# A chunked state-space scan and two feed-forward layers on one core: scores of three tiles from rounded terms, and two edits at the start

## The chip, the cores and the metric

The kernel runs on one NeuronCore of a Trainium2 chip. The metric is the device time of one execution in microseconds (us); lower is better. TensorE (PE) multiplies matrices into PSUM, VectorE (DVE) and ScalarE (ACT) work elementwise, GpSimd (POOL) does a little, SyncE (SP) only issues transfers; ScalarE has a transfer queue of its own.

## The reference

Three stages, each feeding the next, all in float32 from outside:

```python
# 1. chunked scan, per sequence b (4) and head h (8); S=768, D=32, N=16
L = exp(cum_i - cum_j) * causal          # cum: cumulated log a
M = (C_i . B_j) * L                      # the "scores" C_i . B_j, contraction of 16
y = M @ x + (C @ state) * exp(cum)
state = decay * state + sum_j B_j x_j * decay_from_j
# 2. x = y of all heads (3072 x 256)
xn = x / sqrt(mean(x*x) + 1e-6) * rms_g
x2 = (silu(xn @ w_gate) * (xn @ w_val)) @ w_out          # 256 -> 1536 -> 256
# 3. mixes x2 with the row before it
k = relu(xk @ w_k);  v = (k*k) @ w_v;  out = sigmoid(xr @ w_r) * v
```

## The kernel before

The 768 positions are cut into six tiles of 128 (tile c = 0 to 5). A tile holds all 4 sequences, so its feed-forward products have 512 columns. The loop over t runs the feed-forward layers of tile t (`ffn1`: 12 units u, each with products g and v, a Silu, and a contraction x two units later; `ffn2`: 8 units with kp and v), and between the units, at positions given by tables, the scan of tile c = t + 1 (`attend`). Ahead of the loop a list `START` of steps brings in the constants, weights and tile 0's and tile 1's scan.

Every float32 feed-forward product is made of three rounded ones (fp32r: high x high, low x high, high x low; lines 682 to 684). The operands' high parts are casts on ScalarE, the low parts subtractions on VectorE (lines 136, 139). The weights are converted on the way in (`convert`, lines 242 to 285).

Scores: `scores(c, two)` computes C_i . B_j for two sequences at once as plain float32 products. For tiles 2 to 5 (`parity`) there are 16 of 16 rows x 128 columns, four row groups next to each other on the array; for tiles 0 and 1 there are 8 of 32 rows x 256 columns. `SCORES` says in which unit u the two calls stand (tables for t = 0, t = 1 and t from 2 up). `masked` multiplies them with the decays (L472), and `y_two` forms y and the state. The PSUM banks of scores come from the pools `patt` (2 banks) and `pmm` (4, shared with g, v and kp); at the start (`SPARE`) from `patt` and `pacc` (2).

Start of tile 0: `load_a4(0)` brings a, then clip, Ln, scan on VectorE and ScalarE (tile `a`), rounded spread forms (`hv`, `wvvh`, `wkh`), their products `Eb`, Exp to `E`, scores, masks to `M`, y, squares, norms (`tiny`, `xnf`, `xn`), and then the first g. `fill` adds products into an otherwise unused part of a bank behind a step: `FILL` asks for 2 behind the first y, 2 and 3 behind the two norms.

The order of instructions on every engine is not the order of the code: `arrange` runs a list planner (`Order`) over all of them, in program order of priority, with a price for each (`price`, and `costs` for some) and a fixed number of buffers per pool tag. What it gives is fixed as the engine's order; each engine then waits in that order.

Of the kernel before, what the change touches and what calls it, by code (L numbers as in the profile page):

```python
# [16 lines left out]
P = 128  # L17
# [3 lines left out]
NU, NK = DFF // P, DFF2 // P  # L21
T = NB * P

EPS = 5
M8 = 8
GL, SL, CL, SR, CR, ML, MR = 16, 17, 18, 19, 20, 21, 29
KW = 33
# [1 line left out]

SCORES = ((4, 7), (3, 8), (4, 9))
VALUES = ((5, 7, 8, 10), (4, 6, 9, 11), (4, 7, 10, 12))
SCAN = ({3: (4,)}, {0: (0,), 1: (4, 1), 3: (2,), 5: (3,)})

# [7 lines left out]

SUB_DVE, MIX_UNIT = tuple(range(27)), 9
MEANS = (7, 10)
WARM, COLD, HALVED, FILL = (9,), 11, 2, {('y', 0): 2, ('n', 0): 2, ('n', 2): 3}

TABLES = {AF.Ln: "natural_log_exp_and_others", AF.Exp: "natural_log_exp_and_others",
          AF.Silu: "silu_and_others", AF.Sigmoid: "sigmoid_and_others"}
# [5 lines left out]
def shape_constants():  # L55
    p = np.arange(P)
    k = np.zeros((P, KW), np.float32)
    k[:, EPS] = 1e-6
    for h in range(NH):
        k[:, M8 + h] = (p // N) % 4 == h  # L60
    rest, last, head = p % 4 % 2, p % 4 // 2, p // 4 % NH
    k[:, GL] = np.where(rest == 1, -1.0, 0.0)
    seq = p // 32
    k[:, SL], k[:, CL] = np.where(last == 1, -1.0, 0.0), last == 0
    k[:, SR], k[:, CR] = last == 0, last == 1
    for j in range(8):
        k[:, ML + j] = (seq == j // 2) & (head // 4 == j % 2)
    for h in range(4):
        k[:, MR + h] = head % 4 == h
    return k  # L70
# [3 lines left out]
def tile_kernel(ctx: ExitStack, tc, a_c, x_t, B_t, B_s, C_s, B_p, C_p, C_h, kc,  # L74
# [37 lines left out]
    def f32(ap):  # L112
        return ap.bitcast(F32)
# [39 lines left out]
    def kcol(j):  # L153
        return k_sb[:, j:j + 1]
# [180 lines left out]

    a4 = t2("a4").rearrange("p (c i) -> p c i", c=4)[:, :2]

    def load_a4(c):
        nc.sync.dma_start(out=a4[:, c], in_=a_c[c].unsqueeze(1).broadcast_to([32, 4, P]))

    def logs_e(c):
        clip(a4[:, c])
# [51 lines left out]


    def parity(c):
        return c > 1

    def load16(r, src):
        for g in range(4):  # L400
            nc.sync.dma_start(out=r[32 * g:32 * g + N], in_=src[g // 2, N * (g % 2):N * (g % 2) + N])

    def load_b(c, pairs, q):
        if c >= NC:
            return
        if "B4" not in A[c]:
            r = pair("xn", "Br", F32)[:, 0, :] if c == 0 else rp.tile([P, T], F32, tag="Br", bufs=2, name="Br")
            A[c]["B4"] = r.rearrange("p (b x) -> p b x", b=2)
        src = B_p[c].rearrange("r (a b) x -> r a b x", b=2)
        for j in range(2):  # L410
            q.dma_start(out=A[c]["B4"][64 * j:64 * j + 64, pairs], in_=src[:, pairs, j])

    def load_c(c, two, q):
        if c >= NC:
            return
        r = A[c]["C4", two] = rp.tile([P, T], F32, tag="Cr", bufs=2, name="Cr")
        if c > 1:
            load16(r, C_s[c, 2 * two:2 * two + 2])
            return
        q.dma_start(out=r, in_=C_p[c, 2 * two:2 * two + 2].rearrange("b r x -> (b r) x"))  # L420

    def load_bs(c, two):
        if c >= NC:
            return
        r = A[c]["B16", two] = rp.tile([P, T], F32, tag="Br", bufs=2, name="Br")
        load16(r, B_s[c, 2 * two:2 * two + 2])

    def scores(c, two):
        br, cr = A[c].pop(("B16", two)) if parity(c) else A[c]["B4"][:, two], A[c].pop(("C4", two))
        pools = ((patt, "at"), (pacc, "acc") if (c, two) in SPARE else (pmm, "mm"))  # L430
        banks = [[pool.tile([P, T], F32, tag=tag, name="sc") for _ in range(2)] for pool, tag in pools]
        rows, w, n = (N, P, 4) if parity(c) else (2 * N, 2 * P, 2)
        for k in range(n):
            for j in range(4):
                g = slice(32 * j, 32 * j + rows)
                mm = nc.tensor.matmul(banks[j // 2][j % 2][:, k * w:(k + 1) * w], br[g, k * P:(k + 1) * P], cr[g, k * w:(k + 1) * w],  # L436
                                      start=True, stop=True)
                costs[mm.ins.name] = w / 4.0
                if j + k == 0:
                    groups.append((mm.ins.name, [t.name for bank in banks for t in bank]))  # L440
                A[c]["sc", 2 * two + j // 2, j % 2] = banks[j // 2][j % 2]
        if c and two:
            for two in range(2):
                if c + 1 < NC:
                    load_bs(c + 1, two)
                    load_c(c + 1, two, nc.sync)

    def la_scan(c):
        la = A[c]["la"].rearrange("p b i -> p (b i)")
# [24 lines left out]
    def masked(c, b):  # L474
        decayed_b(c, b)
        for half in range(2):
            mask(c, b, half)
# [348 lines left out]
            if len(costs) < COLD:  # L826
                costs[mm.ins.name] = 427.0 if costs else 900.0

    load_a4(0)
    nc.scalar.dma_start(out=k_sb, in_=kc)  # L830
    table(AF.Ln)
    warm_up(WARM[0], patt, "at")
    load_b(0, slice(0, 2), nc.scalar)
# [83 lines left out]
    for t in range(NC):  # L917
        c, e = t + 1, t + 2


        def late(u):
            for b in SCAN[t].get(u, ()):
                if b == 4:
                    la_scan(c)
                    ch_mul(c)
                else:
                    e_scan(c, b)

        def finish(b):
            if b % 2:  # L930
                y_two(c, b - 1)
                for k in range(b - 1, b + 1):
                    if e < NC:
                        load_e(e, k)

        at_sc, at_y = SCORES[min(t, 2)], VALUES[min(t, 2)]

        def attend(u):
            if t <= 1:
                late(u)  # L940
            elif u == 0:
                ch_mul(c)
            if u in at_sc and (c, at_sc.index(u)) not in SPARE:
                two = at_sc.index(u)
                scores(c, two)
                for b in range(2 * two, 2 * two + 2):
                    masked(c, b)
            if u in at_y:
                finish(at_y.index(u))
            if u == NU and e < NC:  # L950
                load_ch(e)
                load_x(e)
            if e < NC:
                if u == 2 and t == 0:
                    a_sb = load_a()
                    clip(a_sb)
                    decays(a_sb)
                if u == 4:
                    load_la(e)
                elif u == 7 and t > 1:  # L960
                    e_scan(e, 0)
                elif u == 9 and t:
                    la_scan(e)
                elif u == 11 and t > 1:
                    e_scan(e, 1)
            if t == 0:
                if u == MEANS[0]:
                    rms_sq(c, cols[0], act_e, vec_e)
                if u == MEANS[0] + 1:
                    rms_mm(c, cols[0])  # L970
                if u == MEANS[1]:
                    rms_sq(c, cols[1], act_e, vec_e)
                    rms_mm(c, cols[1])
                    rms_a(c, full)

        def hook(kind, u):
            if kind == "ab":
                if t == 0:
                    need(NEED[0][u])
                    if u == 0:  # L980
                        for b in range(NB):
                            sf_up(0, b)
                if t == 1:
                    need(NEED[1][u])
                    if u == MIX_UNIT:
                        mix(0, held.pop(0), act_e, vec_e)
                elif t > 1 and u == 0:
                    mix(t - 1, held.pop(t - 1), act_e, vec_e)
                if c < NC:
                    attend(u)  # L990
            if kind == "cd2":
                tail()
            if kind == "cd" and c < NC:
                if t == 1 and u in (1, 2):
                    e_scan(e, u - 1)
                if u == 0:
                    rms_sq(c, full, act_e, vec_e)
                elif u == 3:
                    rms_mm(c, full)
                    rms_a(c, full)  # L1000
                elif u == 4:
                    rms_b(c, full)
                    if e < NC:
                        e_scan(e, 2)
                elif u == 5:
                    xn_out(c, (0,), full, act_e, vec_e)
                    if e < NC:
                        e_scan(e, 3)
                elif u == 6:
                    xn_out(c, (1,), full, act_e, vec_e)  # L1010

        x2, tail = ffn1(t, hook)
        if t == 0:
            tail()
            hook("ab", NU)
            rms_b(c, full)
            xn_out(c, range(2), full, act_e, vec_e)
            x2s = quad("x2s", F32).rearrange("p i a n -> p (i a n)")[:, :2 * NB * (P + 1)]
            x2s = x2s.rearrange("p (m b i) -> p m b i", m=2, b=NB)
            nc.gpsimd.memset(x2s[:, :, :, 0:1], 0.0)  # L1020
            for m in range(2):
                nc.scalar.copy(x2s[:, m, :, 1:], x2[m].rearrange("p (b i) -> p b i", b=NB))
            x2 = [x2s[:, m] for m in range(2)]
        else:
            hook("ab", NU)
            ffn2(t - 1, hook)
        held[t] = x2
# [294 lines left out]
```

## Time and profile before

| | us |
|---|---|
| median of 3 runs | 516.15 (516.13 to 519.57) |
| the profiled execution's own time | 516.75 |
| its span in the trace | 514.70 |
| TensorE busy | 507.2 (99%) |
| VectorE busy | 357.0 (69%) |
| ScalarE busy | 287.4 (56%) |

A profile shows one execution. Busy time of an engine is the union of its instructions' spans; matmuls overlap in a pipeline, so their cost in a dense stretch is read from the distance between starts, not from their length. Times in rows are from the span's start.

### The profile page before, as it was taken

What the parts mean: (1) busy time and instruction counts of PE and PEld (TensorE: products, weight loads), DVE (VectorE), ACT (ScalarE), POOL (GpSimd) and SP (SyncE); (2) the same over time, 40 slices, a digit from 0 to 9 for tenths busy, and PEclk for the clock granted to TensorE, in tenths of its full rate; (3) what the DMA queues carried; (4) which work ended last, traced back from release to release, by engine and by line L of the source; (5) the groups of instructions that cost most, each with busy time, mean ns of one, the idle gap of its engine ahead of it and who ended that gap; (6) DMA issues with size and microseconds to landing.
All of it is one profiled execution on the core that took longest, in us unless ns stands there. A gap on an engine that the chain in (4) does not pass through costs nothing.

```text
span 514.7 us, 7754 instructions
## 1 busy us (share of the span) xinstructions
PE 507.2 (99%) x3023; PEld 409.7 (80%) x3023; DVE 357.0 (69%) x591; ACT 287.4 (56%) x480; POOL 9.2 (2%) x26
## 2 busy tenths in 40 slices
PE   8999999999999999999999999999999999999997
PEld 5687787888888888888888888888888888888885
DVE  5799989989996744769863849854436773335672
ACT  6788779556689623257723257642248652245552
POOL 1100000000010000010000010000001000000000
PEclk9999999999999999999999999999999999999999
DMA  7846666244230102050101231000000010000001
GB/s 256 243 176 203 228 231 234 68 142 138 69 118 1 41 22 81 22 157 28 42 16 43 67 103 41 23 19 1 2 0 1 0 42 0 1 0 2 37 5 42
DMA packets 21477, 37.92 MB, mean 74 GB/s; under 512 B 3760, under 2 KB 7088, under 8 KB 21440
## 3 DMA queue, kind: packets, MB, share of 16 engines
q1 hardware_dynamic: 18704, 28.75, 17.4%
q10 hardware_dynamic: 2736, 8.67, 5.3%
q8 instruction: 24, 0.39, 0.3%
q14 instruction: 13, 0.11, 0.1%
HBM read 33.80 MB, written 3.34 MB: 72 GB/s over the span
## 4 chain that ended last, share of the span: by engine, by line
PE 89%; DVE 6%; ACT 2%; issue 1%; DMA 1%; ACTq 0%; DVEq 0%
PE v L684 10%; PE v L682 10%; PE v L683 10%; PE g L682 6%; PE x L684 6%; PE x L683 6%; PE x L682 6%; PE g L683 6%; PE g L684 6%; PE kp L682 4%; PE kp L684 4%; PE kp L683 4%; PE sc L436 2%; PE y L485 2%; DVE E L459 1%; PE y L527 1%
## 5 line engine op out<-in xcount | busy, mean ns | idle before, releaser
L725 DVE TENSOR_TENSOR hf<-sl,v 128x512 f32<-128x512 f32 x72 | 49.2, 683 | 66.7 <-PE v L684 63.8
L136 ACT CAST h<-hf 128x512 fp32r<-128x512 f32 x72 | 44.5, 620 | 71.1 <-DVE hf L725 69.9
L129 ACT ACTIVATE sl<-g 128x512 f32<-128x512 f32 x72 | 42.4, 594 | 59.5 <-PE g L684 59.5
L139 DVE TENSOR_TENSOR h<-hf,h 128x512 fp32r<-128x512 f32 x72 | 49.2, 687 | 25.1 <-ACT h L136 24.6
L682 PE MATMUL g<-xn,wgh 128*128 128x512 f32 (+1 forms) x148 | 58.8, 398 | 0.0
L683 PE MATMUL x<-h,wol 128*128 128x512 f32 x144 | 56.3, 391 | 0.6 <-DVE wol L285 0.6
L683 PE MATMUL g<-xn,wgl 128*128 128x512 f32 (+1 forms) x148 | 56.9, 384 | 0.0
L684 PE MATMUL g<-xn,wgh 128*128 128x512 f32 (+1 forms) x148 | 56.8, 384 | 0.0
L682 PE MATMUL v<-xn,wvh 128*128 128x512 f32 (+1 forms) x148 | 56.8, 384 | 0.0
L684 PE MATMUL v<-xn,wvh 128*128 128x512 f32 (+1 forms) x148 | 56.8, 384 | 0.0
L683 PE MATMUL v<-xn,wvl 128*128 128x512 f32 (+1 forms) x148 | 56.8, 384 | 0.0
L684 PE MATMUL x<-h,woh 128*128 128x512 f32 x144 | 56.0, 391 | 0.2 <-DVE h L139 0.2
L682 PE MATMUL x<-h,woh 128*128 128x512 f32 x144 | 55.9, 392 | 0.2 <-ACT woh L284 0.2
L139 DVE TENSOR_TENSOR h<-k,h 128x512 fp32r<-128x512 f32 x48 | 32.8, 685 | 14.1 <-ACT h L136 12.5
L136 ACT CAST h<-k 128x512 fp32r<-128x512 f32 x48 | 29.7, 620 | 17.7 <-DVE k L798 17.5
L798 DVE TENSOR_TENSOR k<-rl 128x512 f32<-128x512 f32 x40 | 29.2, 735 | 14.4 <-ACT rl L794 14.4
L682 PE MATMUL kp<-xm,wkh 128*128 128x512 f32 x96 | 37.8, 393 | 0.0
L684 PE MATMUL kp<-xm,wkh 128*128 128x512 f32 x96 | 37.4, 390 | 0.0
L683 PE MATMUL kp<-xm,wkl 128*128 128x512 f32 x96 | 37.4, 389 | 0.0
L684 PE MATMUL v<-h,wvvh 128*128 128x512 f32 x96 | 37.4, 389 | 0.0
L682 PE MATMUL v<-h,wvvh 128*128 128x512 f32 x96 | 37.4, 389 | 0.0
L683 PE MATMUL v<-h,wvvl 128*128 128x512 f32 x96 | 37.4, 389 | 0.0
(147 smaller groups left out, 934.7 us busy)
## 6 DMA issues: line engine op xcount, KB each, us to landing
E<-la_r ACTq DMA_DIRECT2D x16, 512.0 KB
x<-in_x_t SPq DMA_DIRECT2D x6, 512.0 KB
wst<-in_w_gate SPq DMA_DIRECT2D x6, 512.0 KB
wst<-in_w_val SPq DMA_DIRECT2D x6, 512.0 KB
wst<-in_w_out SPq DMA_DIRECT2D x6, 512.0 KB
out<-r SPq DMA_DIRECT2D x12, 256.0 KB
wst<-in_w_k SPq DMA_DIRECT2D x4, 512.0 KB
wst<-in_w_v SPq DMA_DIRECT2D x4, 512.0 KB
```

The costliest lines, as they stand in the source:

```text
L129: one = nc.scalar.activation(out=out, in_=in_, func=func, **kw).ins.name
L136: last[1] = nc.scalar.copy(x[:, 0, :], src).ins
L139: last[0] = le.tensor_tensor(out=x[:, 1, :], in0=src, in1=f32(x[:, 0, :]), op=ALU.subtract).ins
L436: mm = nc.tensor.matmul(banks[j // 2][j % 2][:, k * w:(k + 1) * w], br[g, k * P:(k + 1) * P], cr[g, k * w:(k + 1) * w], start=True, stop=True)
L459: nc.vector.tensor_tensor_scan(out=e, data0=e, data1=cmask, initial=0.0, op0=ALU.mult, op1=ALU.max)
L485: nc.tensor.matmul(y[half][32 * j:32 * j + 32, at[half]:at[half] + P], x[:, b, h * D:(h + 1) * D], m[:, h, :], start=start and at[half] == ...
L527: mm = nc.tensor.matmul(y[half][:, k * P:(k + 1) * P], Sf[g, b + k].rearrange("p h d -> p (h d)"), d["Ch"][g, b + k, :], start=k == 0, sto ...
L682: nc.tensor.matmul(ps[:, s], w[0][:, k, ws], x[:, 0, s], start=first, stop=False, skip_group_check=s.stop - s.start < T)
L683: nc.tensor.matmul(ps[:, s], w[1][:, k, ws], x[:, 0, s], start=False, stop=False, skip_group_check=s.stop - s.start < T)
L684: nc.tensor.matmul(ps[:, s], w[0][:, k, ws], x[:, 1, s], start=False, stop=last, skip_group_check=s.stop - s.start < T)
L725: nc.vector.tensor_mul(hf, sl, v)
L798: nc.vector.tensor_mul(k2, rl, rl)
```

## The change

Four edits. (1) Tiles 3 to 5 (`parity` is now only tile 2) no longer use `scores`. `load_terms` brings one sequence's B and C in four copies on 128 partitions (one transfer each); `terms` rounds them: three activations on ScalarE and three operations on VectorE make `Bs` and `Cs`, which hold high parts and remainders as fp32r; `scores_r` then takes 4 products of 128 rows x 256 columns for one sequence, with the banks of `patt` alone. There are 12 such calls (3 tiles, 4 sequences). The table `SCORES` for t from 2 up has four positions in place of two. (2) The transfer of tile 0's a goes to ScalarE's queue and that of the constants `k_sb` to SP's: they change places. (3) The two filling products behind the first y are gone. (4) The planner's price for the plain score products is doubled (w/2 in place of w/4). The terms' buffers take the tags of tiles that are done by then (`Bs`, `Cs`, `Br`, `Cr`).

```diff
-SCORES = ((4, 7), (3, 8), (4, 9))
+SCORES = ((4, 7), (3, 8), (2, 5, 8, 10))
-... FILL = ... {('y', 0): 2, ('n', 0): 2, ('n', 2): 3}
+... FILL = ... {('n', 0): 2, ('n', 2): 3}
-    def load_a4(c):
-        nc.sync.dma_start(out=a4[:, c], in_=a_c[c].unsqueeze(1).broadcast_to([32, 4, P]))
+    def load_a4(c, q=nc.sync):
+        q.dma_start(out=a4[:, c], in_=a_c[c].unsqueeze(1).broadcast_to([32, 4, P]))
     def parity(c):
-        return c > 1
+        return c == 2
+    def load_terms(c, b):
...
+        for nm, src in (("Br", B_s), ("Cr", C_s)):
+            r = A[c][nm, b] = rp.tile([P, T], F32, tag=nm, bufs=2, name=nm)
+            nc.sync.dma_start(out=r, in_=src[c, b].unsqueeze(0).broadcast_to([4, 32, T]))
+    def terms(c, b):
...
+        nc.scalar.activation(out=bs, in_=br, func=AF.Copy, scale=kcol(SB))
+        for j in range(2):
+            nc.scalar.activation(out=cs[:, :, j, :], in_=cr, func=AF.Copy, scale=kcol(SC0 + j))
+        nc.vector.tensor_add(bs, br, f32(bs))
+        for j in range(2):
+            nc.vector.scalar_tensor_tensor(
+                out=cs[:, :, j, :], in0=cr, scalar=kcol(MC0 + j), in1=f32(cs[:, :, j, :]),
+                op0=ALU.mult, op1=ALU.add)
+        load_terms(c, b + 2)
+    def scores_r(c, b):
...
+        for half in range(2):
+            bank = d["sc", b, half] = patt.tile([P, T], F32, tag="at", name="sc")
+            for q in range(2):
+                p = 2 * half + q
+                nc.tensor.matmul(bank[:, q * 256:(q + 1) * 256], bs[:, p, :],
+                                 cs[:, p, :, :].rearrange("p a i -> p (a i)"), start=True, stop=True)
-                costs[mm.ins.name] = w / 4.0
+                costs[mm.ins.name] = w / 2.0
-    load_a4(0)
-    nc.scalar.dma_start(out=k_sb, in_=kc)
+    load_a4(0, nc.scalar)
+    nc.sync.dma_start(out=k_sb, in_=kc)
-            if u in at_sc and (c, at_sc.index(u)) not in SPARE:
+            if c > 2 and u in (0, 3, 6, 8):
+                terms(c, (u + 1) // 3)
+            if c > 2 and u in at_sc:
+                scores_r(c, at_sc.index(u))
+                masked(c, at_sc.index(u))
+            elif u in at_sc and (c, at_sc.index(u)) not in SPARE:
```

TensorE in the loop, t = 4 (tile 5's scores): first before, where the two calls of a tile each stand as a block of 16 between a contraction x and the next g.

```order
L684 MATMUL x_0_3381<-h,woh 128x512
L682 MATMUL x_1_3382<-h,woh 128x512
L683 MATMUL x_1_3382<-h,wol 128x512
L684 MATMUL x_1_3382<-h,woh 128x512
L436 MATMUL sc<-Cr,Br 128x128 x16
L682 MATMUL g<-xn,wgh 128x512
L683 MATMUL g<-xn,wgl 128x512
```

After (lines 717 to 719 are the old 682 to 684), the first of four groups:

```order
L717 MATMUL v<-xn,wvh 128x512
L718 MATMUL v<-xn,wvl 128x512
L719 MATMUL v<-xn,wvh 128x512
L435 MATMUL sc<-Cs,Bs 128x256 x4
L717 MATMUL g<-xn,wgh 128x512
L718 MATMUL g<-xn,wgl 128x512
```

A block of 16 plain products per two sequences has become two groups of 4 rounded ones; what stands around them is unchanged.

VectorE at the start, before, from the last steps of tile 1's spread (`hv`) to the norms (`tiny`): L472 are tile 0's masks, eight in all; L264, L275 and L285 convert the first weights.

```order
L351 SCALAR_TENSOR_TENSOR hv<-hv,k_sb,a_104 128x128
L472 TENSOR_TENSOR M<-sc,E 128x512
L356 TENSOR_SCALAR hv<-hv,k_sb 128x128 x2
L472 TENSOR_TENSOR M<-sc,E 128x512 x4
L264 TENSOR_SCALAR wst_130<-wst_130 128x1024
L363 TENSOR_TENSOR wvvh<-hv,k_sb 128x512
L275 SCALAR_TENSOR_TENSOR wt_143<-wt_143,wst_130 128x4x128
L363 TENSOR_TENSOR wkh<-hv,k_sb 128x256
L363 TENSOR_TENSOR wkh<-hv,k_sb 128x768
L285 TENSOR_TENSOR wgl<-wt_143,wgh 128x2x128
L285 TENSOR_TENSOR wvl<-wt_143,wvh 128x2x128
L640 TENSOR_SCALAR tiny<-ss 128x2 x2
```

After (line numbers are 5 higher up to 290 and 368, and 35 higher from 507):

```order
L356 SCALAR_TENSOR_TENSOR hv<-hv,k_sb,a_104 128x128
L507 TENSOR_TENSOR M<-sc,E 128x512
L361 TENSOR_SCALAR hv<-hv,k_sb 128x128 x2
L507 TENSOR_TENSOR M<-sc,E 128x512
L368 TENSOR_TENSOR wvvh<-hv,k_sb 128x512
L368 TENSOR_TENSOR wkh<-hv,k_sb 128x256
L507 TENSOR_TENSOR M<-sc,E 128x512 x4
L269 TENSOR_SCALAR wst_130<-wst_130 128x1024
L368 TENSOR_TENSOR wkh<-hv,k_sb 128x768
L280 SCALAR_TENSOR_TENSOR wt_143<-wt_143,wst_130 128x4x128
L675 TENSOR_SCALAR tiny<-ss 128x2
```

Two of tile 1's spread operations now stand between the fourth and the fifth mask, a third ahead of the first merge L280, and the first norm no longer stands behind the low parts of the weights.

## Rows read from the trace of the kernel before

**Rows 1.** Page, part 1: busy us, share of span, instructions.

```profile
PE 507.2 (99%) x3023; PEld 409.7 (80%) x3023; DVE 357.0 (69%) x591; ACT 287.4 (56%) x480; POOL 9.2 (2%) x26
```

**Rows 2.** Windows: length, busy PE, PEld, DVE, ACT, POOL, PEclk, DMA share, GB/s.

```profile
12.50:17.50 5.00, 4.90 (x79) 3.45 (x78) 3.57 (x6) 2.60 (x9) 1.52 (x4) 1.00 1.04 305
12.50:25.00 12.50, 11.54 (x139) 8.06 (x138) 9.40 (x24) 9.91 (x27) 1.52 (x4) 1.00 0.83 244
29.00:150.00 121.00, 119.95 (x803) 96.93 (x803) 114.74 (x179) 86.58 (x136) 1.61 (x4) 1.00 0.50 161
150.00:385.00 235.00, 235.00 (x1446) 192.17 (x1444) 152.68 (x245) 115.96 (x192) 2.69 (x3) 1.00 0.13 40
```

**Rows 3.** Timeline of PE around tile 5's first scores: start, length, instruction.

```profile
345.74 0.39 PE L684 MATMUL x<-h,woh 128*128 128x512 f32 x1
346.06 1.17 PE L436 MATMUL sc<-Cr,Br 16*128 16x128 f32 x32
347.16 0.50 PE L682 MATMUL g<-xn,wgh 128*128 128x512 f32 x1
347.50 0.40 PE L683 MATMUL g<-xn,wgl 128*128 128x512 f32 x1
```

**Rows 4.** Timeline of PE, rounded products of 256, then 512 columns.

```profile
28.94 0.28 PE L683 MATMUL g<-xn,wgl 128*128 128x256 f32 x1
...
34.57 0.40 PE L682 MATMUL g<-xn,wgh 128*128 128x512 f32 x1
...
39.81 0.39 PE L684 MATMUL v<-xn,wvh 128*128 128x512 f32 x1
```

**Rows 5.** Groups of instructions by line: total busy, mean ns.

```profile
L139 DVE TENSOR_TENSOR h<-hf,h 128x512 fp32r<-128x512 f32 x72 | 49.2, 687 | 25.1 <-ACT h L136 24.6
L757 DVE SCALAR_TENSOR_TENSOR xf<-x,om,p 128x508 f32<-128x508 f32 x20 | 14.0, 740 | 0.0
L756 ACT ACTIVATE p<-x,k_sb 128x512 f32<-128x512 f32 x20 | 12.9, 683 | 0.9 <-DVE carry L766 0.9
```

**Rows 6.** Timeline of PE around the first y; in brackets idle before, releaser.

```profile
11.06 0.64 PE L485 MATMUL y<-M,x 128*32 128x128 f32 x16
11.63 1.13 PE L571 MATMUL ss<-ones 128*128 128x256 f32 x4
12.69 1.15 PE L436 MATMUL sc<-Cr,Br 32*128 32x256 f32 x16
```

**Rows 7.** Timeline of DVE around the masks of tile 0.

```profile
11.24 0.68 DVE L472 TENSOR_TENSOR M<-sc,E 128x512 f32<-128x512 f32 x1
11.85 0.59 DVE L356 TENSOR_SCALAR hv<-hv,k_sb 128x128 fp32r<-128x128 f32 x2
13.93 2.48 DVE L472 TENSOR_TENSOR M<-sc,E 128x512 f32<-128x512 f32 x4 [1.49 <-PE sc L436]
```

**Rows 8.** Timeline of DVE, its later waits ahead of the first g.

```profile
18.51 0.69 DVE L275 SCALAR_TENSOR_TENSOR wt<-wt,wst 128x512 int32<-128x512 int32 x1 [0.90 <-ACT wt L269]
...
21.00 0.43 DVE L285 TENSOR_TENSOR wgl<-wt,wgh 128x256 fp32r<-128x256 f32 x1 [0.59 <-ACT wgh L284]
...
25.77 1.66 DVE L664 SCALAR_TENSOR_TENSOR xnf<-yT,k_sb,ss 128x256 f32<-128x256 f32 x4 [0.74 <-PE ss L571]
```

**Rows 9.** Timeline of PE, its last two waits of the start.

```profile
21.82 0.38 PE L376 MATMUL Eb<-before,eye 128*128 128x512 bf16 x1 [0.85 <-ACT E L129]
...
41.76 0.50 PE L683 MATMUL x<-h,wol 128*128 128x512 f32 x1 [0.62 <-DVE wol L285]
```

**Rows 10.** Timeline of the start: the two transfers and who waits for them.

```profile
0.73 0.38 ACTq L830 DMA_DIRECT2D k_sb<-in_kc  x1
...
0.73 0.68 SPq L339 DMA_DIRECT2D a<-in_a_c  x1
...
2.48 0.24 DVE L165 TENSOR_SCALAR om<-k_sb 128x2 f32<-128x2 f32 x2 [1.47 <-DMA k_sb<-in_kc]
...
3.93 0.23 DVE L182 TENSOR_SCALAR a<-a 128x128 f32<-128x128 f32 x1 [1.21 <-DMA a<-in_a_c]
```

More of the change, by code (lines that the diff above doesn't have):

```diff
@@ L22 @@
 T = NB * P
-EPS = 5
+SB, SC0, SC1, MC0, MC1, EPS = range(6)
 M8 = 8
@@ L45 @@
 MEANS = (7, 10)
-WARM, COLD, HALVED, FILL = (9,), 11, 2, {('y', 0): 2, ('n', 0): 2, ('n', 2): 3}
+WARM, COLD, HALVED, FILL = (9,), 11, 2, {('n', 0): 2, ('n', 2): 3}
 TABLES = {AF.Ln: "natural_log_exp_and_others", AF.Exp: "natural_log_exp_and_others",
@@ L58, in shape_constants @@
     k[:, EPS] = 1e-6
+    term, h2 = p // 32, (p // 16) % 2
+    k[:, SB] = np.where(term >= 2, -1.0, 0.0)
+    for j in range(2):
+        k[:, MC0 + j] = h2 == j
+        k[:, SC0 + j] = np.where((term % 2 == 1) & (h2 == j), -1.0, 0.0)
     for h in range(NH):
@@ L396, in parity @@
     def parity(c):
-        return c > 1
+        return c == 2
+    def load_terms(c, b):
+        if b >= NB:
+            c, b = c + 1, b - NB
+        if c >= NC:
+            return
+        for nm, src in (("Br", B_s), ("Cr", C_s)):
+            r = A[c][nm, b] = rp.tile([P, T], F32, tag=nm, bufs=2, name=nm)
+            nc.sync.dma_start(out=r, in_=src[c, b].unsqueeze(0).broadcast_to([4, 32, T]))
+    def terms(c, b):
+        d = A[c]
+        bs = d["Bs", b] = rp.tile([P, 4, P], F32R, tag="Bs", bufs=1, name="Bs")
+        cs = d["Cs", b] = rp.tile([P, 4, 2, P], F32R, tag="Cs", bufs=1, name="Cs")
+        br, cr = (d.pop((nm, b)).rearrange("p (k i) -> p k i", k=4) for nm in ("Br", "Cr"))
+        nc.scalar.activation(out=bs, in_=br, func=AF.Copy, scale=kcol(SB))
+        for j in range(2):
+            nc.scalar.activation(out=cs[:, :, j, :], in_=cr, func=AF.Copy, scale=kcol(SC0 + j))
+        nc.vector.tensor_add(bs, br, f32(bs))
+        for j in range(2):
+            nc.vector.scalar_tensor_tensor(
[3 more added lines that the diff above has]
+    def scores_r(c, b):
+        d = A[c]
+        bs, cs = d.pop(("Bs", b)), d.pop(("Cs", b))
+        for half in range(2):
[4 more added lines that the diff above has]
+                                 cs[:, p, :, :].rearrange("p a i -> p (a i)"), start=True, stop=True)
     def load16(r, src):
@@ L403, in load_b @@
     def load_b(c, pairs, q):
-        if c >= NC:
-            return
         if "B4" not in A[c]:
@@ L413, in load_c @@
     def load_c(c, two, q):
-        if c >= NC:
-            return
         r = A[c]["C4", two] = rp.tile([P, T], F32, tag="Cr", bufs=2, name="Cr")
@@ L422, in load_bs @@
     def load_bs(c, two):
-        if c >= NC:
-            return
         r = A[c]["B16", two] = rp.tile([P, T], F32, tag="Br", bufs=2, name="Br")
@@ L443, in scores @@
             for two in range(2):
-                if c + 1 < NC:
+                if c == 1:
                     load_bs(c + 1, two)
                     load_c(c + 1, two, nc.sync)
+                else:
+                    load_terms(c + 1, two)
     def la_scan(c):
```

## Prediction

> **What bounds the kernel now.** I read the page's busy times first, then the windows by stretch, then the timeline of TensorE, and last the timeline of VectorE where TensorE has gaps. The page shows TensorE busy 99%, VectorE 69%, ScalarE 56% [rows 1]. The windows split this into two regimes. From 150 to 385 us TensorE is busy in all of 235 us, VectorE in 152.7 [rows 2]: time there changes only by what TensorE has to do. From 29 to 150 us TensorE is busy 119.95 of 121 us, but VectorE 114.7 [rows 2]: it is nearly a second bound. Ahead of 29 us neither is steady. There a chain runs through all engines, and what it gains or loses goes one to one to the end, as long as TensorE is dense behind it: its last wait is the one at 41.76 us, for a weight's low part from VectorE [rows 9]. So three questions decide: what the scores cost TensorE, whether the new work of VectorE and ScalarE is hidden, and by how much the start shortens.
>
> **Scores on TensorE.** A rounded product of 512 columns starts 0.228 us behind the one before: from 34.57 to 39.81 us are 23 steps [rows 4]. Around the block of tile 5's first scores the last x product starts at 345.74 and the second g product at 347.50 us [rows 3], 1.76 us apart, where without the block it would be two steps, 0.46. A block costs 1.30 us; tiles 3 to 5 have six like it, 7.8 us. In place of each come 8 rounded products of 256 columns. Between 28.94 and 34.57 us stand 47 steps of such products, 0.120 us each, the step into the 512-column ones included [rows 4]. So 12 groups of 4 cost 48 x 0.120 = 5.8 us, and TensorE saves 2.1 us. Bounds: a plain block pays 0.09 us on entry (0.32 less 0.228) and 0.11 on exit (0.34 less 0.228) [rows 3]; did each of the 12 new groups pay the same 0.20, the saving would be a loss of 0.3. I take 2.1, since the new products are of the same kind as their neighbours and the step from 256 to 512 columns in rows 4 shows nothing extra.
>
> **Terms on VectorE and ScalarE.** Per sequence VectorE gets one addition and two scalar_tensor_tensor operations, 0.687 + 2 x 0.740 = 2.2 us, and ScalarE three scaled copies of 0.683, 2.0 us [rows 5]; for 12 sequences 26 and 25 us. Eleven of the 12 lie behind 150 us, where VectorE has 82 us free and ScalarE 119 [rows 2]. The order shows them a whole step ahead of the products that read them (the first sequence's terms of a tile stand in the tile before), so I cost them at nothing; without that cover each would be a wait of 2.2 us. The one sequence of tile 3 whose terms stand ahead of 150 us takes 2.2 of the 6.3 us that VectorE has free from 29 to 150 [rows 2]. Fewer but larger transfers (24 of 256 KB for 48 of 32 KB) run where the transfers' share is 0.13 [rows 2]; on SP's queue they wait for a buffer like the small ones did, with the next tile's loads and the output behind them, all due many units later. Nothing. Pool `pmm` is no longer borrowed from g and v, but TensorE is busy without a gap in this stretch [rows 2], so that gives nothing either.
>
> **The start: filling products.** The two behind the first y run from 11.63 to 12.69 us, 1.06 us, directly ahead of tile 0's second scores [rows 6]. They don't come free as a whole. The second scores need all four banks, and the last is released by the fourth mask. In the order before that mask ends at 11.92 (11.24 + 0.68) and two `hv` steps follow to 12.44 [rows 7]; in the new order the same operations stand ahead, but the `hv` steps stand before the fourth mask, so it ends near 12.45. The scores then end near 13.5 in place of 13.8: of 1.06 us some 0.25 is left, and TensorE waits instead.
>
> **The start: order on VectorE.** This is the larger part. Up to its last norm step VectorE waits four times for long: 1.49 us ahead of the fifth mask [rows 7], 0.90, 0.59 and 0.74 us [rows 8], in sum 3.7. In the new order `wvvh` and the first `wkh` (0.6 + 0.35 us by distance of starts) move into the first wait and leave 0.25. The large `wkh` comes ahead of the merge that waited 0.90, and the norms come ahead of the low parts that waited 0.59. New waits come up: for ScalarE ahead of the second norm (0.4 us, as ScalarE now does two Exps and two casts first), 0.15 for a cast, and about 0.9 for the three filling products behind the second norm, which stay. That is 1.7 where 3.7 stood. VectorE is then 2.0 us ahead; from there to the low parts of w_out, for which TensorE waits at 41.76 [rows 9], both orders hold nearly the same work, so that wait ends 2.0 us earlier too. The estimate rests on the chain walked through by hand with the durations of before. Bounds: 0 if other waits eat it, 3.7 if all four vanish.
>
> **The start: two queues.** Both transfers are issued at 0.73 us, one on each queue; the constants are used at 2.48, a at 3.93 [rows 10]. If a had the constants' speed on the other queue it would land 1.45 us earlier. But its issue takes 0.68 us where that of the constants takes 0.38 [rows 10], and it moves more bytes, wherever it is issued. I take 0 (nearest is its own row), with 1.45 us of gain as one bound; the other is a loss of 0.4, if the table load and issues on ScalarE hold it up by as long as the constants' issue. The Trainium skill (DMA: Bandwidth & Descriptors, "Issuing engines are not separate DMA queues") says that transfers of all issuing engines share the same 16 DMA engines and that another issuer saves only sequencer time; by that the sum would stay as it is, while the row of the constants taken alone would make it 1.45 us better.
>
> **Sum.** 2.1 + 2.0 = 4.1 us. The profiled execution took 516.75 us, 2.05 more than its span and 0.6 more than the median of the runs; against the median of 516.15 the forecast is 512.1 us, 0.8% faster. About 1% (5.2 us, so 511.0) is what a measurement of this kernel can tell from no change.
>
> **Rivals.** *The lead of the start is lost*: VectorE is busy 114.7 of 121 us behind it [rows 2], and with 2.2 us of terms 4.1 us are free; if its later work comes when TensorE already asks for it, TensorE waits, and only the scores' 2.1 us remain: 514.1. For it speaks that VectorE is the releaser of the last wait [rows 9]; against it that TensorE shows no wait behind 42 us at the same load. *A lands with the other queue's speed*: 1.45 us more, 510.6. For it the constants' row, against it the length of the issue [rows 10]. *The scores save nothing*, because groups of 4 pay an entry and exit as the blocks do: 0.3 lost in place of 2.1 gained, 514.5; the change then does not do what it says.
>
> *Slower, through the clock*: the filling products kept TensorE occupied; without them it waits about 0.9 us at 11.6. The granted clock is 1.00, that is 2.4 GHz, in every start window [rows 2], through a wait of 0.85 us at 21.8 too [rows 9]; that speaks against it. If it fell to 1.2 GHz there, the products between 12.5 and 17.5 us (4.9 us busy) would take 4.9 us more, those up to 25 us 11.5 more [rows 2]: 517.0 to 523.6. It decides from 4.1 us of products at the lower clock on. The Trainium skill (TensorE: Matmul & The Clock Gate, "A second HAM failure mode: psum-queue depth-cycling") describes a kernel whose TensorE went back and forth between its two clocks as it idled briefly between groups of matmuls that cycle through PSUM banks; by that page this wait for a bank could bring the fall, though no window of this trace shows one.
>
> **How the numbers follow.** Forecast 512.1 (own range 511.2 to 513.2): 0.42. Lead lost, 514.1 (513.2 to 514.7): 0.25. A early, 510.6: 0.18. Scores save nothing, 514.5: 0.09. Slower through the clock: 0.06. The range for 8 in 10 reaches from 510.3, a little under the early a, to 515.0, a little over the scores' bound; it leaves out the clock, and ends of both sides. Faster by over 1%, under 511.0: 0.19, the early a and the best of the forecast's start; slower by over 1%: 0.04; within: 0.77.
>
> **What would show it.** Right: groups of 4 products with starts 0.12 us apart and no wait around them in tiles 3 to 5, a tile's scores costing TensorE 1.9 us in place of 2.6; VectorE's first `xnf` some 4 us ahead of 25.77 [rows 8], and the wait for the low part of w_out ending near 39.8; clock 1.00 throughout. Wrong: a wait of TensorE for `Cs` or `sc`; VectorE as releaser of waits between 42 and 150 us; a granted clock under 1.00 in the first 30 us; a used much before or after 3.93.

## The result and the profile after

The changed kernel takes 521.16 us (median of 8 runs, 518.54 to 523.18), the kernel before 516.76 beside it: a ratio of 1.0077 with a 95% interval of 1.0056 to 1.0099. It is slower by 0.8%, where 512.1 had been forecast. The profiled execution took 521.35 us, its span is 519.3.

The page of the kernel after, parts 1 and 2 (first line busy time, second the granted clock in 40 slices); it answers to [rows 1]:

```profile
PE 508.1 (98%) x2875; PEld 410.4 (79%) x2875; DVE 377.6 (73%) x627; ACT 308.4 (59%) x516; POOL 9.5 (2%) x26
...
PEclk9999999899999999999999999999999999999999
```

TensorE has 148 products fewer and yet is busy 0.9 us longer. The 8th slice holds the one stretch where its clock fell. Windows of the kernel after, columns as in [rows 2]:

```profile
12.50:25.00 12.50, 12.43 (x142) 8.97 (x138) 10.05 (x25) 9.89 (x29) 1.89 (x4) 1.00 0.70 194
...
29.00:150.00 121.00, 115.49 (x761) 90.78 (x760) 109.18 (x175) 84.78 (x131) 0.71 (x4) 0.99 0.54 169
...
150.00:385.00 235.00, 234.95 (x1276) 193.91 (x1275) 175.75 (x280) 135.87 (x228) 3.57 (x4) 1.00 0.18 59
...
85.00:100.00 15.00, 12.30 (x49) 9.50 (x48) 13.50 (x24) 8.53 (x15) 0.00 (x0) 0.89 0.38 119
```

Up to 25 us TensorE is busier than before, behind 150 us as dense. From 29 to 150 us it lost 4.46 us of busy time (119.95 to 115.49). So the loss sits where the scores of tiles 3 to 5 are not, and 85 to 100 us, with a granted clock of 0.89, hold 2.5 us of it (14.78 us busy before, 12.30 after); what the lower clock costs comes on top, since slow products count as busy. Timeline of TensorE in the kernel after; it answers to [rows 3, 9]:

```profile
35.49 0.50 PE L717 MATMUL v<-xn,wvh 128*128 128x512 f32 x1 [1.26 <-ACT sl L134]
...
40.88 0.50 PE L718 MATMUL x<-h,wol 128*128 128x512 f32 x1 [0.41 <-DVE wol L290]
...
44.59 0.47 PE L717 MATMUL v<-xn,wvh 128*128 128x512 f32 x1 [0.48 <-ACT sl L134]
...
90.24 0.38 PE L689 MATMUL rb<-tiny 128*128 128x128 f32 x2
93.31 0.50 PE L717 MATMUL g<-xn,wgh 128*128 128x512 f32 x1 [2.69 <-ACT xn L141]
...
94.57 0.48 PE L718 MATMUL g<-xn,wgl 128*128 128x512 f32 x1
94.85 0.63 PE L717 MATMUL v<-xn,wvh 128*128 128x512 f32 x1
...
97.84 0.55 PE L719 MATMUL g<-xn,wgh 128*128 128x512 f32 x1
98.22 0.39 PE L718 MATMUL v<-xn,wvl 128*128 128x512 f32 x1
...
134.51 0.50 PE L717 MATMUL g<-xn,wgh 128*128 128x512 f32 x1 [0.50 <-DVE E L507]
...
342.63 0.39 PE L719 MATMUL v<-xn,wvh 128*128 128x512 f32 x1
342.86 0.64 PE L435 MATMUL sc<-Cs,Bs 128*128 128x256 f32 x4
343.33 0.40 PE L717 MATMUL g<-xn,wgh 128*128 128x512 f32 x1
343.56 0.40 PE L718 MATMUL g<-xn,wgl 128*128 128x512 f32 x1
```

Read it from below. A group of four new score products takes 342.86 to 343.33, 0.47 us or four steps of 0.12, with nothing extra on either side. Above it stands the wait for a mask (0.50 us), and at 93.31 the one that decides: the first gate product of t = 1 waits 2.69 us for tile 1's normed input. The first products behind it still start 0.23 us apart (93.65 to 94.57); then the steps grow to 0.43: from 94.57 to 98.22 are 9 steps in 3.65 us that take 2.05 at the high level, 1.6 us lost. Over 94.7 to 98.2 us the granted clock is 0.51, so these steps are those of the lower of TensorE's two levels (1.2 of 2.4 GHz).

I compared the start of the same product in both traces (after less before): the first 512-column g -2.0 us (34.57 to 32.56), an x product at 51 us +0.2, the last x product of tile 0 +0.4, an x product at 98 us +5.15, at 131 us +5.98, the first r product in t = 2, 3, 4 +5.35, +5.05, +4.4. These numbers say where everything went: the first 512-column g comes 2.0 us earlier as forecast, that is gone by 45 us, 4.7 us are lost between tiles 0 and 1, 0.8 at 131 us, and the scores give 1.6 us back (5.98 to 4.4).

Timeline of VectorE in the kernel after, its first use of a, tile 0's norms, the boundary between the tiles, and the first terms:

```profile
3.68 0.23 DVE L187 TENSOR_SCALAR a<-a 128x128 f32<-128x128 f32 x1 [2.67 <-DMA a<-in_a_c]
...
20.95 0.87 DVE L699 SCALAR_TENSOR_TENSOR xnf<-yT,k_sb,ss 128x256 f32<-128x256 f32 x2 [0.48 <-PE ss L606]
...
23.56 0.87 DVE L699 SCALAR_TENSOR_TENSOR xnf<-yT,k_sb,ss 128x256 f32<-128x256 f32 x2 [1.23 <-PE ss L606]
...
88.48 0.69 DVE L144 TENSOR_TENSOR h<-hf,h 128x512 fp32r<-128x512 f32 x1
89.08 0.69 DVE L269 TENSOR_SCALAR wst<-wst 128x1024 f32<-128x1024 f32 x1
89.68 2.28 DVE L494 TENSOR_TENSOR_SCAN E<-E,cmask 128x1024 f32<-128x1024 f32 x1
91.89 0.72 DVE L699 SCALAR_TENSOR_TENSOR xnf<-yT,k_sb,rb 128x512 f32<-128x512 f32 x1
92.52 1.22 DVE L280 SCALAR_TENSOR_TENSOR wt<-wt,wst 128x1024 int32<-128x1024 int32 x1
93.66 0.74 DVE L699 SCALAR_TENSOR_TENSOR xnf<-yT,k_sb,rb 128x512 f32<-128x512 f32 x1
...
113.33 0.69 DVE L421 TENSOR_TENSOR Bs<-Br,Bs 128x512 fp32r<-128x512 f32 x1 [2.64 <-ACT Bs L418]
```

Between the last `h` of tile 0 and tile 1's `xnf` stand a clip and an E scan of tile 2, 2.8 us, and a merge between the two `xnf`. In the kernel before the same h was followed at once by `xnf` (88.32 us), the scan came at 94.54:

```profile
87.12 1.28 DVE L139 TENSOR_TENSOR h<-hf,h 128x512 fp32r<-128x512 f32 x2
88.32 0.74 DVE L664 SCALAR_TENSOR_TENSOR xnf<-yT,k_sb,rb 128x512 f32<-128x512 f32 x1
...
94.54 2.28 DVE L459 TENSOR_TENSOR_SCAN E<-E,cmask 128x1024 f32<-128x1024 f32 x1
```

TensorE's first g product of t = 1 started there at 89.83 us, 0.24 us behind the last x product.

### The profile page after: what moved, and what is told of

It is laid out like the page before. It is cut to its first block, busy times and chain, and to the rows that moved or that the text cites. A ratio compares the mean times of both kernels' runs of the same rounds, so it can differ in the third digit from the quotient of the medians.

```text
span 519.3 us, 7513 instructions
## 1 busy us (share of the span) xinstructions
PE 508.1 (98%) x2875; PEld 410.4 (79%) x2875; DVE 377.6 (73%) x627; ACT 308.4 (59%) x516; POOL 9.5 (2%) x26
## 4 chain that ended last, share of the span: by engine, by line
PE 79%; DVE 11%; DMA 4%; ACT 3%; issue 2%; ACTq 0%; SPq 0%; DVEq 0%
PE v L717 9%; PE v L719 9%; PE v L718 9%; PE g L717 5%; PE g L718 5%; PE g L719 5%; PE x L718 5%; PE x L717 5%; PE x L719 5%; PE kp L717 4%; PE kp L719 4%; PE kp L718 4%; DVE E L494 3%; PE y L520 2%; DVE wt L280 2%
## 5 line engine op out<-in xcount | busy, mean ns | idle before, releaser
L494 DVE TENSOR_TENSOR_SCAN E<-E,cmask 128x1024 f32<-128x1024 f32 x16 | 36.6, 2289 | 2.0 <-DMA E<-la_r 2.0
```

The costliest lines, as they stand in the source:

```text
L494: nc.vector.tensor_tensor_scan(out=e, data0=e, data1=cmask, initial=0.0, op0=ALU.mult, op1=ALU.max)
```

## The experiments

**Which edit.** Four kernels: the changed one with the old price (e1), and the kernel before with one part alone (e2: price, e3: terms and scores, e4: queues and no filling products).

```diff
# e1, in the changed kernel
-  costs[mm.ins.name] = w / 2.0
+  costs[mm.ins.name] = w / 4.0
# e2, in the kernel before
-  costs[mm.ins.name] = w / 4.0
+  costs[mm.ins.name] = w / 2.0
# e3: the changed kernel with w / 4.0, both old queues and ('y', 0): 2 in FILL
# e4, in the kernel before
-  FILL = {('y', 0): 2, ('n', 0): 2, ('n', 2): 3}
+  FILL = {('n', 0): 2, ('n', 2): 3}
-  load_a4(0); nc.scalar.dma_start(out=k_sb, in_=kc)
+  load_a4(0, nc.scalar); nc.sync.dma_start(out=k_sb, in_=kc)
```

e1: 

> The changed kernel with the planner's price of the plain score products put back to w/4; everything else stays changed. Theory A (the doubled price moves an E scan ahead of tile 1's xnf, so TensorE waits 2.7 us at 93.31 us and its clock falls behind that): order and time of tile 0 are as before, the 1.95 us of the scores and up to 0.25 us of the earlier a remain, some 2.0 to 2.3 us below the kernel before, about 514.6; no wait above 1 us between 85 and 100 us, clock 1.00. Theory B (the rounded terms, their loads and their work on VectorE cost the time) and theory C (the two queues or the missing filling products cost it): as the changed kernel, some 4.4 us above the kernel before, about 521.

e2: 

> The kernel before with the doubled price w/2 alone. Theory A: the lead of 2 us at the start, then the wait before tile 1's first gate products and the lower clock; without the scores' 1.95 us it is the slowest of all, some 6 us above the kernel before, about 522.8, with a TensorE wait of 2 to 3 us near 93 us. Theories B and C: no change, or up to 2 us faster by the shorter start, 514.8 to 516.8.

e3: 

> The kernel before with the rounded terms and their scores for tiles 3 to 5 alone (old price, old queues, the two filling products kept). Theory A and theory C: 1.95 us below the kernel before, about 514.8. Theory B: some 4 us above it, about 521.

e4: 

> The kernel before with a on ScalarE's queue, the constants on SP's and without the two filling products behind the first y; old price, old scores. Theory A and theory B: within 0.5 us of the kernel before (0.25 us from a at most), 516.3 to 516.8. Theory C: 4 to 6 us above it.

Measured beside 516.81 us of the kernel before: e1 515.26 (ratio 0.9970, 0.9960 to 0.9980), e2 521.12 (1.0091, 1.0068 to 1.0113), e3 515.11 (0.9974, 0.9963 to 0.9986), e4 516.23 (0.9986, 0.9973 to 0.9998). Theory A holds, B and C fall: the doubled price alone makes the kernel slower, by 4.3 us (6 were expected), and without it the other edits make it faster. The window 85 to 100 us of the kernel before, of e1 and then of e2:

```profile
85.00:100.00 15.00, 14.78 (x81) 11.57 (x83) 14.79 (x24) 10.18 (x18) 0.11 (x1) 1.00 0.10 29
```

```profile
85.00:100.00 15.00, 14.81 (x95) 11.87 (x95) 15.00 (x23) 10.47 (x18) 0.12 (x1) 1.00 0.13 31
```

```profile
85.00:100.00 15.00, 12.31 (x56) 9.61 (x56) 15.00 (x26) 9.59 (x16) 0.00 (x0) 1.00 0.36 106
```

In e2 TensorE misses the same 2.7 us as in the changed kernel, but the clock stayed at 1.00 in this execution, which took 519.3 us, the shortest of e2's six. The five others took 520.6 to 523.4 us, with a mean granted clock of 0.993 to 0.997 over the whole execution; that fits a fall of the clock in them, but no trace of them shows where. e1 and e3 beat both kernels.

**The wait and the clock.** e5 marks tile 1's norm urgent in the changed kernel, so that the planner keeps VectorE free for it; e6 fills the wait with 12 products; e7 doubles the price for tile 0 alone; e8 is the changed kernel with the old queues and filling products.

```diff
# e5, at the end of t = 0
+  at = len(list(nc.cur_bb.bb.instructions))
   rms_b(c, full)
   xn_out(c, range(2), full, act_e, vec_e)
+  urgent.extend(i.name for i in list(nc.cur_bb.bb.instructions)[at:] if ...)
# e6, ahead of the first g of t = 1, chained behind the last x of t = 0
+  for _ in range(12):
+      mm = nc.tensor.matmul(gv[n, u], ones, <ones, 512 columns>, start=True, stop=True)
# e7
+  costs[mm.ins.name] = w / (2.0 if c == 0 else 4.0)
```

e5: 

> The changed kernel with tile 1's norm (rms_b and xn_out of t = 0) marked urgent for the planner, so that on VectorE the two xnf and the two xn stand together, ahead of the E scan and of the merge wt; the order up to there is that of the changed kernel. Theory A1 (the wait there costs 2.7 us and the lower clock behind it some 1.7 us more): both go, 4.4 us less than the changed kernel, about 516.8; no TensorE wait above 0.5 us between 85 and 100 us and a granted clock of 1.00 in 85 to 100 (0.89 in the changed kernel). Theory A2 (the order before that point has cost the time already, and the wait only hides work that comes later): 1 us less at most, above 520.

e6: 

> The changed kernel with 12 products of 512 columns (2.6 us at the high clock), whose results nobody uses, put on TensorE between the last product of t = 0 and the first gate product of t = 1; the order of VectorE and ScalarE around them is that of the changed kernel. If the clock falls because TensorE had no products for 3.1 us: xn comes at the same time as in the changed kernel, the gate products behind it start 0.228 us apart, the granted clock in 85 to 100 is 1.00, and the time is 1 to 1.7 us less, 519.5 to 520.2. If the clock falls for another reason: unchanged, 521.2, or a little above where the filling delays xn's consumers.

e7: 

> The changed kernel with the price doubled for the plain score products of tile 0 alone (w/4 for tiles 1 and 2). VectorE's order in tile 0 and so the lead of 2 us at the start stay, while at the end of t = 0 xnf again stands ahead of the E scan. Theory A1: no long wait and no lower clock at 93 us, 515 to 517, and what is left of the lead shows at the first product of t = 1. Theory A2: 519 or more.

e8: 

> The changed kernel with the old queues and with the two filling products behind the first y; terms and doubled price stay. The three edits measured alone gave +4.3 (price), -1.7 (terms) and -0.6 us (queues and filling). If they add: 516.8 + 4.3 - 1.7 = 519.4. If the late transfer of w_out (issued at 26.8 us in the changed kernel, at 21.3 us under the doubled price alone) comes from the queues or the missing filling products, the ScalarE wait of 1.3 us before wst at 33.8 us is gone as well. If they don't add, as the changed kernel, about 521.

Measured beside 517.10 us: e5 516.10 (0.9982, 0.9964 to 0.9999), e6 519.65 (1.0051, 1.0036 to 1.0066), e7 519.05 (1.0040, 1.0025 to 1.0054), e8 520.37 (1.0072, 1.0046 to 1.0099). e5 gives back 4.9 us by the two ratios, as A1 says; timeline of TensorE in e5, without a long wait and with steps of 0.23 us behind it:

```profile
89.80 0.39 PE L719 MATMUL x<-h,woh 128*128 128x512 f32 x1
90.31 0.50 PE L717 MATMUL g<-xn,wgh 128*128 128x512 f32 x1
90.64 0.40 PE L718 MATMUL g<-xn,wgl 128*128 128x512 f32 x1
90.88 0.40 PE L717 MATMUL v<-xn,wvh 128*128 128x512 f32 x1
```

Timeline of TensorE in e6, the 12 filling products and what follows:

```profile
91.70 3.01 PE L740 MATMUL g<-ones 128*128 128x512 f32 x12
94.65 0.50 PE L717 MATMUL g<-xn,wgh 128*128 128x512 f32 x1
94.98 0.39 PE L718 MATMUL g<-xn,wgl 128*128 128x512 f32 x1
95.21 0.39 PE L717 MATMUL v<-xn,wvh 128*128 128x512 f32 x1
```

The input comes no earlier, but the steps behind it are 0.23 us: between the last x product and the one at 98 us e6 loses 3.15 us, the changed kernel 4.72. So 1.6 us of that were the clock, and with products in the wait it did not fall. That it fell because TensorE had no products is what this speaks for; one profile does not exclude chance, since e2 kept 1.00 with the wait unfilled, as e8 did. All six runs of e6 have a mean granted clock of 0.999 or 1.000, the eight of the changed kernel 0.992 to 1.000. The whole time of e6 (1.3 us less by the two ratios) is a mix: in its profile the first x product already comes 1.3 us later (41.00 to 39.73), and the mask's wait at 134 us is missing. e7 misses: 519.05 us lies where theory A2 had put it. Its trace shows what A1 says at the boundary, no long wait and a granted clock of 1.00 from 85 to 100 us. But its lead too is lost (from -0.2 us at the first 512-column g to +2.1 at an x product near 47 us of the kernel before), and its profiled first g comes 2.0 us behind the changed kernel's (the last section); so e7 by its time supports neither theory. e8 can't tell whether the three edits add: its interval holds both their sum (519.4 beside 516.8, a ratio of 1.0050) and the changed kernel's 1.0077. ScalarE's wait for w_out at 33.8 us is gone in it without the lead staying.

**The same wait in the kernel before.** In the kernel before, e9 chains tile 2's last E scan ahead of tile 1's first `xnf` and marks that norm urgent.

```diff
 nc.vector.tensor_tensor_scan(out=e, data0=e, data1=cmask, ...)
+if (c, b) == (2, 3): chains.append((<this scan>, <first xnf of tile 1>))
```

> The kernel before (old price, old scores, old queues) with one thing changed by hand: on VectorE the last E scan of tile 2 has to stand ahead of tile 1's first xnf; with it the planner puts there wst, Ch and two Bd, some 3.8 us of work in all, and the two xnf behind it. Theory A1 (such work ahead of xnf is what costs the time, whatever the price is): TensorE waits 3 to 4.5 us for xn near 92 us, and the clock may fall behind that; 3 to 6 us above the kernel before, 520 to 523. Theory A2 (the wait hides time that is lost anyway elsewhere): within 1 us of the kernel before.

Measured: 524.84 us beside 516.90 (1.0146, 1.0131 to 1.0160), 7.9 us more, above the expected 3 to 6. Timeline of TensorE in e9:

```profile
88.97 0.50 PE L685 MATMUL x<-h,woh 128*128 128x512 f32 x1 [0.99 <-ACT h L136]
...
94.95 0.79 PE L685 MATMUL g<-xn,wgh 128*128 128x512 f32 x1 [4.32 <-ACT xn L136]
95.54 0.63 PE L686 MATMUL g<-xn,wgl 128*128 128x512 f32 x1
...
100.66 0.57 PE L686 MATMUL g<-xn,wgl 128*128 128x512 f32 x1
101.07 0.39 PE L687 MATMUL g<-xn,wgh 128*128 128x512 f32 x1
```

A wait of 4.32 us, one of 0.99 ahead of it, and 14 steps from 94.95 to 101.07 us in 6.12 us that take 3.2 at the high level: 2.9 us, in sum 8.2. (The granted clock of 85 to 100 us is 0.81.) The wait was about as expected, the clock cost more. The mechanism needs neither the price nor the terms.

**Where the lead goes between 33 and 45 us.** All four start from e5. e10 chains tile 1's decay scan behind the low parts of the next `w_gate` and `w_val`; e11 leaves out three clips on VectorE; e12 is e11 with the old price; e13 chains the weight steps of that stretch into the order of before.

```diff
# e10, in la_scan(1)
+  chains.append((<last wl of weight pair 6>, <this scan>))
# e11, e12, in move(); e12 also w / 4.0
+  if j in (4, 6, 8): return
# e13, besides e10's chain
+  <clip 6> before <merge 4>; <first ScalarE step of 6> before <woh, wol>; <merge 6> before <wol>
```

e10: 

> The changed kernel with tile 1's norm urgent, as in the experiment before, and with tile 1's decay scan (1.23 us on VectorE) chained behind the low parts of the second third of w_gate and w_val, as it stood in the kernel before. If the lead of 2 us is lost between 33 and 45 us because that scan and Ch stand ahead of those weights: most of 1.9 us comes back, 514.2 to 515.0, and the first y of tile 1 comes 2.5 us or more ahead of the 62.4 us of the kernel before. If it is lost because VectorE has no free time there at all and only other work gets late: as without the chain, 516.1.

e11: 

> The changed kernel with tile 1's norm urgent, and without the clipping of the third, fourth and fifth pair of weight blocks to the largest finite value (line L264 of the kernel before: three operations of 0.69 us on VectorE between 34 and 60 us are left out; on finite weights they change nothing). Theory V (the lead is lost because VectorE has no free time from 29 to 85 us, so whatever is put later there is waited for): 1.8 us less of VectorE's work keeps most of the 1.7 us of lead, 514.2 to 514.8, first y of tile 1 at 60.4 to 61.2 us. Theory O (single operations stand in an unlucky order, however much work there is): no better than with the clipping, 515.7 to 516.5.

e12: 

> The same with the old price w/4, so with VectorE's order of the start as in the kernel before and no lead there; the clipping of the same three pairs is left out. Theory V: TensorE waits only 0.8 us in 35 to 45 us with the old order, so the same 1.8 us of VectorE's work brings 0.8 us at most against the 515.26 us of the changed kernel with the old price: 514.5 to 515.3, and it ends no earlier than the kernel with the doubled price and without clipping. Theory O: 515.3, and 1 us or more below that kernel.

e13: 

> The changed kernel with tile 1's norm urgent, and with the conversion of the second w_out and the next w_gate and w_val blocks chained into the order of the kernel before on VectorE and ScalarE (both clips and both merges ahead of wol, wol ahead of wgl and wvl, tile 1's decay scan behind them). If the lead of the start was lost in 33 to 45 us through the order of these steps: TensorE waits there some 0.8 us as in the kernel before, the first y of tile 1 comes 1.5 us or more ahead of the 62.4 us of the kernel before, and the time is 514.2 to 515.0. If the lead goes whatever their order (the steps take VectorE and ScalarE until then in any order): first y within 0.8 us of 62.4 us, and 515.7 to 516.8.

Measured: e10 516.60 beside 516.90 (1.0006, 0.9986 to 1.0025); e11 519.19 and e12 521.74 beside 516.39 (1.0050, 1.0031 to 1.0069; 1.0106, 1.0082 to 1.0129); e13 518.84 beside 516.55 (1.0030, 1.0012 to 1.0049). None kept the lead. In e10 the last x products of that stretch still come 1.75 us ahead of before, the first g product with `wgl` behind them (44.11 us) only 0.28. Taking work off VectorE made things worse, with the old price too: in e11 and e12 TensorE waits 3.4 and 2.7 us near 45 us, and the granted clock of 45 to 60 us is 0.89 in both. Timeline of TensorE in e11:

```profile
44.87 0.50 PE L719 MATMUL g<-xn,wgh 128*128 128x512 f32 x1 [3.45 <-ACT sl L134]
```

So theory V as I tested it falls, and theory O's times are missed as well: with three operations fewer the planner makes another order (in e11 VectorE's decay scan of tile 1 stands at 33.73 us, in e5 at 36.15), and that order costs more than the work. e13 excludes least: its first 512-column g came at 36.13 us, 1.6 us behind the kernel before, at a low clock (the last section). By the first x product with `wol` it was 3.2 us behind, waiting 1.09 us for `woh` and 0.69 for `wol` where the kernel before waits 0.20 and 0.62.

## Why the prediction was wrong

**Scores on TensorE**: right. Four steps of 0.12 us, no entry or exit. By the r products of t = 2 to 4 a tile gains 0.64, 0.29 and 0.65 us in the changed kernel and 1.92 in sum in e3, where 2.1 was forecast. The 0.29 has one step of 0.44 us at 320.96 in it. The trace names no releaser for it, but the v product behind it is the one that in e5 waits 0.40 us for VectorE's `h` (316.31 us). As a measured time e3 gave 1.7 us by the medians and 1.3 by the ratio (0.7 to 1.9). The rival by which the scores save nothing is out.

**Terms on VectorE and ScalarE**: right behind 150 us but for that one step (no wait for `Cs` or `sc`), wrong for the one sequence ahead of it. I had costed the transfers at nothing. In the changed order tile 3's first `Br` is issued at 106.0 us, and ScalarE stands 4.43 us for it, VectorE 2.64 behind ScalarE; the masks of tile 2 then come late, and TensorE loses 0.8 us at 131 us (134.51 in the kernel after). Other kernels with the terms show the same in measure: a wait for `Br` of 4.74 us and then one of 0.73 for the mask in e8, 2.52 and 0.39 in e7, 1.27 and none in e5. Timeline of ScalarE in the kernel after, here and at its wait in the start:

```profile
33.80 1.16 ACT L276 ACTIVATE wst<-wst 128x1024 int32<-128x1024 uint32 x1 [1.26 <-DMA wst<-in_w_out]
...
112.57 0.72 ACT L418 ACTIVATE Bs<-Br,k_sb 128x512 fp32r<-128x512 f32 x1 [4.43 <-DMA Br<-in_B_s]
```

In e1 and e3 the same transfer is issued at 100 us and nobody waits for it; there the forecast of nothing holds. The first row is the wait behind which `sl` stood, and with it TensorE's 1.26 us at 35.49.

**The start: two queues and filling products**: right, at nothing. a is used at 3.68 us in place of 3.93 [rows 10], but that is no gain of the queue: over all traces the first use lies at 3.27 to 3.31 us in four of the five executions with the old queue and at 3.33 to 3.85 in the ten with the new one, and the kernel before happened to be profiled with the late 3.93. The first use in e9 (old queue), then in e4 (new):

```profile
3.27 0.23 DVE L182 TENSOR_SCALAR a<-a 128x128 f32<-128x128 f32 x1 [0.55 <-DMA a<-in_a_c]
```

```profile
3.33 0.23 DVE L182 TENSOR_SCALAR a<-a 128x128 f32<-128x128 f32 x1 [2.32 <-DMA a<-in_a_c]
```

So the 1.45 us rival is out. The Trainium skill's rule cited there (DMA: Bandwidth & Descriptors, "Issuing engines are not separate DMA queues") agrees. Both edits alone (e4) measured 0.6 us faster with an interval that almost reaches no change (0.9998); counted from a's first use, e4's first 512-column g comes 0.1 us earlier than in the kernel before.

**The start: order on VectorE**: the failed step. Its first half is right: of VectorE's long waits (3.7 us before) 0.36, 0.48 and 1.23 are left, 2.1 in place of the forecast 1.7, and the lead at 32.56 us is 2.0 us. That it is exactly the forecast is partly luck: 0.25 of it is a's late landing in the trace of before. Counted from a's first use the lead is 1.8 us, and in e2, with the price alone, 1.1. Its second half, that from there "both orders hold nearly the same work, so that wait ends 2.0 us earlier too", is wrong, and so is what the section on the bound says, that a gain goes to the end as long as TensorE is dense behind it. The wait for `wol` ended at 40.88 in place of 39.8, and by 45 us nothing was left. I had walked the order up to 42 us and taken the rest as unchanged. It was not: the doubled price moved an E scan ahead of tile 1's norm, 45 us later, and that cost a wait of 2.7 us and 1.6 us of the lower clock. Shown by e2 (the price alone does it), e5 (that norm put first, 4.9 us come back), e6 (the clock's share, in one profile) and e9 (the same in the kernel before). Why the planner sets this order at that price was only read from the order, not tested.

The rival of the lost lead (514.1) had the loss right and took the rest as unchanged as well; its sign of trouble, VectorE as releaser between 42 and 150 us, is what came, at 134.51 us directly and at 93.31 through ScalarE's `xn`.

**Slower, through the clock**: that a wait lowers the clock was right, the edit that brings it, the place and the cost were wrong. Behind 11.6 us the clock held in the changed kernel, 1.00 in all windows up to 85 us; it fell behind the 2.7 us wait at 93 us, which comes from the price and not from the missing filling products. The rival was not empty, though: of the ten profiled executions without those products two (e4 and e13) fell to the lower level between 17 and 24 us, of the five with them none. That is too few to show a cause, and in e4 TensorE was busy in all of the 6 us from 12 to 18, just ahead of the fall. The section I had cited (the Trainium skill, TensorE: Matmul & The Clock Gate, "A second HAM failure mode: psum-queue depth-cycling") speaks of short idling between groups; no run here shows that it lowered the clock, and what did in e4 and e13 stays open. Nearer is "HAM oscillation — how this bites in real kernels" of the same page of the Trainium skill, where a wait for the next tile's input makes the clock fall; e6 and e9 agree, only that here the input comes from VectorE and ScalarE, not from a transfer, and that in e2 and e8 a wait as long brought no fall.

**The sum** against the forecast of -4.1 us, by the traces: lead lost 2.4 (2.0, and 0.4 beyond it), boundary 4.7, mask 0.8, scores 0.5 less than forecast. That is 8.4, so +4.3, beside +4.4 at the last products and +4.6 of the profiled executions.

**Open**: what takes the lead between 33 and 45 us. Every kernel with the doubled price loses it; the place of the decay scan, less work on VectorE and the order of the weight steps did not keep it, and none of them left the rest of the order alone.

## What to carry to other kernels

A planner's price is not a local edit: it can reorder all engines far from what it prices, so it is timed by itself, and the old and new order are compared to the end, first of all at each place where TensorE changes from one tile to the next. There the question is what stands on the slower engine between the last product's input and the next tile's first. Here a wait of TensorE of 2.7 us cost 1.6 us more through the clock, one of 4.3 us 2.9 more, and in the profiled executions of e2 and e8 the 2.7 us cost nothing more; a forecast of a wait gives both cases a chance. And a lead of 2 us between two profiled executions is read from a common event (here the first use of a), since the start itself shifts by more than half a us from one execution to the next.

## What the runs showed of the hardware that was not expected

- Equal waits, unequal clocks. After a wait of 2.69 us the changed kernel's products stayed at the lower level for some 3.4 us (94.74 to 98.15 in the trace's clock record), which cost 1.6 us; e2 and e8, with waits of 2.68 and 2.67 us, kept 1.00 in their profiled executions. After 4.32 us e9 stayed low longer, 14 steps in place of 9, and from its first product on.
- A low clock need not cost its whole price. In e4's profiled execution the granted clock was 0.50 between 19 and 21 us (low from 18.1 to 21.5). There e4 lost only 0.3 us against the kernel before, which in that stretch waits 0.85 us for `E` [rows 9] where e4 does not. In e13 the clock was low for twice as long (17.1 to 23.9 us), VectorE waited 2.78 us for TensorE's `ss`, and the first g came 3.6 us behind the changed kernel's (28.93 to 25.37); 0.7 of that was there at the first y. Windows of e4 and e13, and VectorE in e13:

```profile
19.00:21.00 2.00, 2.00 (x17) 1.18 (x9) 1.40 (x7) 2.00 (x6) 0.00 (x0) 0.50 0.30 81
```

```profile
12.50:25.00 12.50, 12.46 (x110) 8.48 (x102) 8.22 (x21) 8.90 (x25) 1.69 (x4) 0.73 0.67 200
```

```profile
24.52 0.87 DVE L711 SCALAR_TENSOR_TENSOR xnf<-yT,k_sb,ss 128x256 f32<-128x256 f32 x2 [2.78 <-PE ss L618]
```

- The same first products can take 0.71 or 1.19 us for a pair: in e6 and e7 those at 6.7 us and the score block behind them (8.78 to 10.74 us in e6, where the changed kernel takes 1.1) ran slow until 10.7 us, and the first g came some 2 us later than in the changed kernel, with the same order of TensorE up to there. The clock's rise fits that: the trace's clock record opens, at the high level, at 10.62 us in e6 and 10.36 in e7, in all other traces between 4.1 and 6.9. Ahead of its first record a window reads 1.00 whatever the steps show (6 to 11 us in e6), so at a kernel's start the clock is read from the steps.
